# Seven block products for the second product of three feature groups, and one width for all token pairs

## The chip, the cores and the metric

The kernel runs on one core of a Trainium2 chip. The metric is the device time of one execution in microseconds; the kernel before takes 845.44 us (median of 3 runs, 845.15 to 845.78).

## What is computed

Sparse attention over 4 batches x 8 heads x 576 tokens (head size 64; half of the heads see a local window, half a strided set), then two feed-forward layers on the 2304 x 512 result, each with 2048 features, in float32:

```python
attn = np.exp(scores); attn = attn / (np.sum(attn, axis=-1, keepdims=True) + 1e-09)
x = (attn @ v), heads side by side               # 2304 x 512
h = x @ w_in;  g = h * np.clip(h + 3.0, 0.0, 6.0) / 6.0;  x = g @ w_out      # layer 1
h = x @ w_in;  g = h * np.tanh(softplus(h));              x = g @ w_out      # layer 2
```

## The kernel before, in words

Everything is held transposed: features or channels on the 128 partitions, tokens along the free dimension. `xs[0..3]` are the four 128-channel blocks of x, and later of y. A float32 operand is split into a high part (rounded to fp32r) and a low part (the rest), and each block product is a *triple* of matmuls in `mm3` (lines 985 to 987): low weights x high data, high x low, high x high.

**Order of the work.** Every instruction is first added to a `Plan` as an `Op` with its engine (or several to choose from), a cost, what it depends on, a due time and perhaps a PSUM bank. `Plan.run` then places them one by one, and the instructions are emitted in that order; each engine runs its own list in order. The constants at the top (`START`, `SOON`, `OVERLAP`, `EARLY_X`, `UNIT_Y`, `LEAD`, `BIAS`) move due times and choices in this plan.

**Stages.** Attention of 16 head pairs is mixed with the *plain steps*: the first 4 feature blocks of layer 1, by ordinary products, over all tokens in five stretches (`PLAIN`). Their y goes to DRAM (`y_kept`). From about 170 us on come 21 *units* (`build`). A unit is one of three token pairs (`TOKENS`: 2 x 288, 2 x 432 and 2 x 432 tokens) and two pairs of feature blocks (`u.fs`, two values of `fp`). Layer 1 (m = 0) has 3 groups, layer 2 (m = 1) has 4, each of 3 units.

**First product, seven products.** x as 2 x 2 blocks (two token halves, two channel halves) and w_in as 2 x 2 blocks are multiplied by Winograd's form with 7 block products instead of 8 (`PRODUCTS`: a11, a12, s2, s1, s4, s3, a22). `x_operands` makes the seven operands from `xs` in a layer's first group, splits them and keeps them in DRAM (`kept`); later groups load them (5 buffers). `decode` unpacks the packed float64 weights on VectorE (`unpack`, 512 columns at a time), makes four differences, mostly on GpSimd (line 868), and splits the pieces into `win`. A product is 2 triples (q) per fp. Partial sums stay in the bank: s2 is added onto a11's bank after a copy of it has been taken out, then s1, then s4; a22 onto s3's. So TensorE waits there for the copy or the add (lines 1179 and 1197) of the product before.

**Activation and split.** `result` (line 1108 on) applies the activation and `split` (line 763 on) makes the high part (a cast, mostly ScalarE, line 341) and the low part (a subtraction, VectorE or GpSimd, line 769) in one of 8 g tiles.

**Second product, plain.** For each token half t and each of the 4 output blocks d, one bank takes 4 triples in a row (two fp, two blocks j), then one add onto y (line 1249; line 1238 with the y kept in DRAM for layer 1's first group; a copy for layer 2's):

```python
for t in range(2):
    for d in range(KC):
        for k, (fp, j) in enumerate(chain):    # 4 triples into one bank
        ...
        o = add("dve", ..., nc.vector.tensor_tensor(y(), src(), y(), ALU.add), ...)
```

So a unit has 28 triples in the first product and 32 in the second. Banks 0 to 3 serve the first product, 4 to 7 the second (`BANKS`); in the profile and the order their names are bank_61 to 64 and bank_65 to 68. xs_75 to 78 are the four output blocks, win and wout the weights of the first and second product. Outputs of the last group go to DRAM by the SP queue as they are done.

## Time and profile before

| | us |
|---|---|
| median of 3 runs (lowest, highest) | 845.44 (845.15, 845.78) |
| the profiled execution | 847.64 |
| its span, first to last instruction | 845.9 |
| TensorE busy | 834.4 (99%) |
| VectorE busy | 588.7 (70%) |
| ScalarE busy | 421.1 (50%) |
| GpSimd busy | 225.2 (27%) |

PE is TensorE, PEld its weight loads, DVE VectorE, ACT ScalarE, POOL GpSimd, SP the queue that issues the DMAs. Matmuls are pipelined: the duration of one is longer than the distance to the next, and a full share does not say that TensorE is at its peak. A group's row ends with the time the engine stood idle just before its instructions, and whom it waited for.

### The profile page before, as it was taken

How to read it: one execution, taken by the hardware profiler on the slowest of the kernel's cores; microseconds unless marked ns; L12 is line 12 of the kernel's file. 1: busy time of each engine (PE TensorE's matmuls, PEld its weight loads, DVE VectorE, ACT ScalarE, POOL GpSimd, SP SyncE). 2: the span in 40 equal slices, each digit the busy share in tenths (PEclk: the TensorE clock that was granted, in tenths of full speed). 3: DMA queues.
4: the chain of work that ended last, by engine and by line, in shares of the span. 5: the costliest groups of instructions: out<-in, count | busy, mean ns of one | idle time of the engine just before them, and what ended most of it. 6: DMA issues, size and time to landing. Idle time of an engine off the chain costs nothing.

```text
span 845.9 us, 16976 instructions
## 1 busy us (share of the span) xinstructions
PE 834.4 (99%) x6760; PEld 774.8 (92%) x6760; DVE 588.7 (70%) x1108; ACT 421.1 (50%) x876; POOL 225.2 (27%) x237
## 2 busy tenths in 40 slices
PE   7899999999999999999999999999999999999998
PEld 4577888899999999999999999999999999999998
DVE  4688876789988868879879989766537762423423
ACT  2667766577454443544355775643353352432512
POOL 4443213424434331422304533302012300100101
PEclk8899999999999999999999999999999999999999
DMA  8866652477887876668843677757655873645731
GB/s 241 239 198 214 194 173 77 156 263 259 281 289 248 293 260 224 232 210 285 283 172 140 233 257 237 250 188 275 248 172 175 272 273 101 210 157 197 246 130 68
DMA packets 85219, 182.31 MB, mean 216 GB/s; under 512 B 6036, under 2 KB 65044, under 8 KB 85140
## 3 DMA queue, kind: packets, MB, share of 16 engines
q1 hardware_dynamic: 84480, 181.06, 63.6%
q8 instruction: 53, 0.87, 0.4%
q10 hardware_dynamic: 660, 0.16, 0.1%
q14 instruction: 26, 0.21, 0.1%
HBM read 138.74 MB, written 42.47 MB: 214 GB/s over the span
## 4 chain that ended last, share of the span: by engine, by line
PE 97%; DMA 1%; ACT 1%; issue 0%; DVE 0%; ACTq 0%; POOL 0%; SPq 0%; DVEq 0%
PE bank L985 30%; PE bank L986 30%; PE bank L987 30%; PE bank L708 2%; PE bank L1270 1%; PE bank L602 1%; PE bank L669 1%; DMA v<-in_qkv_dram 1%; DMA mk_str<-in_masks_dram 1%; PE bank L671 0%; ACT pt L341 0%; ACTq L508 0%; ACT xs L341 0%; ACT v L568 0%; POOL e L660 0%
## 5 line engine op out<-in xcount | busy, mean ns | idle before, releaser
L985 PE MATMUL bank<-x,win 128*128 128x432 f32 (+3 forms) x668 | 229.6, 344 | 0.1
L986 PE MATMUL bank<-x,win 128*128 128x432 f32 (+3 forms) x668 | 227.9, 341 | 0.0
L987 PE MATMUL bank<-x,win 128*128 128x432 f32 (+3 forms) x668 | 227.7, 341 | 0.0
L985 PE MATMUL bank<-g,wout 128*128 128x432 f32 (+3 forms) x416 | 144.2, 347 | 0.0
L987 PE MATMUL bank<-g,wout 128*128 128x432 f32 (+3 forms) x416 | 142.8, 343 | 0.0
L986 PE MATMUL bank<-g,wout 128*128 128x432 f32 (+3 forms) x416 | 142.7, 343 | 0.0
L1249 DVE TENSOR_TENSOR xs<-bank,xs 128x432 f32<-128x432 f32 (+1 forms) x120 | 66.7, 556 | 107.7 <-PE bank L987 106.8
L985 PEld LDWEIGHTS bank<-x,win 128*128 128x128 f32 x668 | 125.5, 188 | 7.0 <-POOL win L769 0.7
L986 PEld LDWEIGHTS bank<-x,win 128*128 128x128 f32 x668 | 125.8, 188 | 5.6 <-POOL x L769 0.5
L987 PEld LDWEIGHTS bank<-x,win 128*128 128x128 f32 x668 | 125.6, 188 | 5.5
L769 POOL TENSOR_TENSOR g<-t,g 128x432 fp32r<-128x432 f32 (+3 forms) x44 | 47.4, 1082 | 264.9 <-ACT g L341 165.5
L985 PE MATMUL bank<-g_late,wout 128*128 128x432 f32 (+1 forms) x336 | 113.1, 336 | 0.0
L986 PE MATMUL bank<-g_late,wout 128*128 128x432 f32 (+1 forms) x336 | 113.0, 336 | 0.0
L987 PE MATMUL bank<-g_late,wout 128*128 128x432 f32 (+1 forms) x336 | 112.9, 336 | 0.0
L987 PEld LDWEIGHTS bank<-g,wout 128*128 128x128 f32 x416 | 78.2, 188 | 4.5
L985 PEld LDWEIGHTS bank<-g,wout 128*128 128x128 f32 x416 | 78.3, 188 | 4.0
L986 PEld LDWEIGHTS bank<-g,wout 128*128 128x128 f32 x416 | 78.2, 188 | 3.5
L341 ACT COPY c<-bank 128x432 f32<-128x432 f32 (+1 forms) x42 | 20.0, 482 | 108.1 <-PE bank L987 108.1
L987 PEld LDWEIGHTS bank<-g_late,wout 128*128 128x128 f32 x336 | 63.2, 188 | 1.7
L985 PEld LDWEIGHTS bank<-g_late,wout 128*128 128x128 f32 x336 | 63.2, 188 | 1.6
L986 PEld LDWEIGHTS bank<-g_late,wout 128*128 128x128 f32 x336 | 63.2, 188 | 1.6
L769 DVE TENSOR_TENSOR g<-t,g 128x432 fp32r<-128x432 f32 (+2 forms) x60 | 39.1, 656 | 27.9 <-ACT g L341 27.5
(105 smaller groups left out, 1273.4 us busy)
## 6 DMA issues: line engine op xcount, KB each, us to landing
x<-kept SPq DMA_DIRECT2D x70, 864.0 KB, 5.0
raw<-in_wts_dram SPq DMA_DIRECT2D x64, 512.0 KB, 5.7
kept<-x SPq DMA_DIRECT2D x28, 864.0 KB, 4.7
x<-kept SPq DMA_DIRECT2D x35, 576.0 KB, 4.8
qk<-in_qkv_dram SPq DMA_DIRECT2D x14, 576.0 KB, 5.7
kept<-x SPq DMA_DIRECT2D x14, 576.0 KB, 2.8
v<-in_qkv_dram SPq DMA_DIRECT2D x14, 432.0 KB, 7.8
y<-keep SPq DMA_DIRECT2D x16, 256.0 KB, 2.1
```

The lines of the kernel that those rows point to most:

```text
L341: nc.scalar.copy(out, src)
L602: nc.tensor.matmul(banks[both[h].n][g * QN:(g + 1) * QN, slot * WK:(slot + 1) * WK], src.q[h * D:(h + 1) * D, n // 6, n % 2 * QN:(n % 2 + ...
L669: nc.tensor.transpose(banks[turned[0].n][:, j * P:(j + 1) * P], e[:, t:t + 2].rearrange("p s k -> p (s k)"), ident)
L708: nc.tensor.matmul(o[h * D:(h + 1) * D], src.v[rows, NB + others(local).index(n) if n in others(local) else i, h * D:(h + 1) * D], pt[rows ...
L769: lambda eng: engines[eng].tensor_tensor(lo(), src(), hi().bitcast(F32), ALU.subtract),
L985: nc.tensor.matmul(o, low_w, high, start=first, stop=False, skip_group_check=True)
L986: nc.tensor.matmul(o, high_w, low, start=False, stop=False, skip_group_check=True)
L987: nc.tensor.matmul(o, high_w, high, start=False, stop=last, skip_group_check=True)
L1249: "dve", dve_ns(n), lambda y=y, src=src: nc.vector.tensor_tensor(y(), src(), y(), ALU.add),
L1270: plan.filler = cleared, 3 + 4 * FILL / 2.4, lambda n: nc.tensor.matmul(banks[n][:, :FILL], zeros[:, :P], zeros, start=True, stop=True)
```

## The change

Three things change together.

1. `TOKENS` becomes 3 x (2 x 384) instead of 2 x 288, 2 x 432, 2 x 432, and `WIDE` 384; operand buffers are now without gaps. `PLAIN` becomes 512, 448, 512, 320, 512.
2. The seven products get a new order (`PRODUCTS`), and in it another use of the banks (`CHAIN`): a12 has its own bank, and a copy of it is taken first; s3 and a22 share one; a11, s2, s1 and s4 share one. The activated blocks stay in the buffers c, u, v and t instead of passing through t.
3. Groups 2 to 4 of layer 2 (`BOTH`) form the second product by seven block products too. `decode` treats their output weights like the input weights (four differences, 28 block columns). `g_operand` makes s3, s1, s2 and s4 from the activated blocks and splits seven operands per fp. Each product is then 2 triples (one per fp) for each of 2 output blocks q, in the order `SECOND`, and after each product its bank's running sum is added onto y (line 1295). A bank is used on before it is free: the next product of its chain waits for that add. Of units without it, the second token half now comes first.

The diff, cut to its core (buffers, names and the records of who uses a buffer are left out):

```diff
-TOKENS = ((0, 288), (576, 432), (1440, 432))
-WIDE = 448
-PLAIN = (512, 512, 512, 256, 512)
+TOKENS = ((0, 384), (768, 384), (1536, 384))
+WIDE = 384
+PLAIN = (512, 448, 512, 320, 512)
...
+BOTH = ((0, 0, 0), (0, 1, 1, 1))
-PRODUCTS = ("a11", "a12", "s2", "s1", "s4", "s3", "a22")
+PRODUCTS = ("a12", "a11", "s3", "s2", "a22", "s1", "s4")
+SECOND = ("a11", "s3", "s2", "a22", "s1", "a12", "s4")
+CHAIN = {"a11": "a", "s2": "a", "s1": "a", "s4": "a", "a12": "c", "s3": "b", "a22": "b"}
...
-N_OUT, N_OUT_EARLY = 4, 2
-N_X, X_FROM = 5, 3
+N_OUT, N_OUT_EARLY = 3, 2
+N_X = 5
+N_G, N_G_EARLY = 9, 6
-N_RAW, N_WA, N_T, N_F, N_S = 3, 2, 3, 2, 2
+N_RAW, N_WA, N_T, N_F = 2, 2, 3, 4
+N_S = {"c": 2, "u": 2, "v": 2}
...
-START, FIRST_PACE = 42117, 3359
+START, FIRST_PACE = 42920, 3359
-SOON = 54
+SOON = 11
-OVERLAP = 9536
-UNIT_Y, UNIT_X = -740, 15237
-LEAD = 0.6776
+OVERLAP = 14375
+UNIT_Y, UNIT_X = 6429, 15237
+LEAD = 1.0667
-BIAS = {"act": -347, "dve": 300, "pool": 0}
+BIAS = {"act": -305, "dve": 318, "pool": 0}
...
-        u.one, u.two = 7 * cost, 8 * cost
+        u.one, u.two = 7 * cost, (7 if u.both else 8) * cost
...
+        def chain_of(keys, use, before, product, evict, first_due):
...
+            banks_of = {(c, key): Bank(use) for c in "abc" for key in keys}
+            last, gone = {}, {}
+            for i, kind in enumerate(PRODUCTS if use == "h" else SECOND):
+                c = CHAIN[kind]
+                for key in keys:
+                    bank, started = banks_of[c, key], (c, key) in last
+                    deps = [*last.get((c, key), []), *gone.get((c, key), [])]
...
+                    last[c, key] = [prev]
+                    gone[c, key] = evict(i, kind, key, prev, bank, lambda bank=bank: banks[bank.n][:, :n])
...
+        def g_operand(fp, name, number):
+            if name == "s3":
+                summed(fp, "s3", "a11", "a21", ALU.subtract)
+            elif name == "s2":
+                summed(fp, "s1", "a21", "a22", ALU.add)
+                summed(fp, "s2", "s1", "a11", ALU.subtract)
+            elif name == "s4":
...
+                    lambda eng: engines[eng].tensor_tensor(x.tile(), x.tile(), y.tile(), ALU.subtract),
...
+            ops = split(n, lambda: g_tiles(slot)[0], lambda: g_tiles(slot)[1], r.tile, r.ready, old)
...
+            TO = {"a11": (0, 0), "s3": (1, 1), "s2": (1, 0), "a22": (1, 0), "s1": (1, 1), "a12": (0, 0), "s4": (0, 1)}
+            def second_evict(i, kind, q, o, bank, psum):
...
+                (t, c), ends = TO[kind], kind in ("a22", "a12", "s4")
+                return add_to_y(t, 2 * q + c, o, psum, due + UNIT_Y, bank if ends else None, kind in ("a22", "a12", "s4", "s1"))
+            before = opened["y"][-2:]
+            chain_of(range(2), "y", before, second_product, second_evict, u.at + u.one)
+            return
...
-        for t in range(2):
+        for t in (1, 0):
```

**How the order moves, TensorE.** Within the last group of layer 2, before, where the next unit's first product (x,win) stands beside a unit's second product (g_late,wout):

```order
L985 MATMUL bank_65<-g_late,wout_72 128x432
L986 MATMUL bank_65<-g_late,wout_72 128x432
L987 MATMUL bank_65<-g_late,wout_72 128x432
L985 MATMUL bank_62<-x,win_2287 128x432
L986 MATMUL bank_62<-x,win_2287 128x432
L987 MATMUL bank_62<-x,win_2287 128x432
L985 MATMUL bank_64<-x,win_69 128x432
L986 MATMUL bank_64<-x,win_69 128x432
L987 MATMUL bank_64<-x,win_69 128x432
L985 MATMUL bank_68<-g_late,wout_71 128x432
L986 MATMUL bank_68<-g_late,wout_71 128x432
L987 MATMUL bank_68<-g_late,wout_71 128x432
```

and the same place of the change:

```order
L1012 MATMUL bank_67<-g,wout_2289 128x384
L1013 MATMUL bank_67<-g,wout_2289 128x384
L1014 MATMUL bank_67<-g,wout_2289 128x384
L1012 MATMUL bank_63<-x,win_2288 128x384
L1013 MATMUL bank_63<-x,win_2288 128x384
L1014 MATMUL bank_63<-x,win_2288 128x384
L1012 MATMUL bank_67<-g,wout_71 128x384
L1013 MATMUL bank_67<-g,wout_71 128x384
L1014 MATMUL bank_67<-g,wout_71 128x384
L1012 MATMUL bank_63<-x,win_2288 128x384
L1013 MATMUL bank_63<-x,win_2288 128x384
L1014 MATMUL bank_63<-x,win_2288 128x384
```

Before, triples of the two products stand in ones and twos, with long runs of one alone elsewhere (57 matmuls of the second product, 45 of the first in a unit of this group). Now single triples of the two alternate through most of layer 2, and a bank of the second product (65, then 67) is left after two triples, one per weight buffer, for the next bank.

**How the order moves, VectorE.** The end of its list, the last unit, before (t_87 and g_late belong to the operands' split, xs_75 to 78 are the output blocks):

```order
L769 TENSOR_TENSOR g_late<-t_87,g_late 128x288
L1249 TENSOR_TENSOR xs_75<-bank_65,xs_75 128x288
L1249 TENSOR_TENSOR xs_76<-bank_68,xs_76 128x288
L1249 TENSOR_TENSOR xs_77<-bank_66,xs_77 128x288
L1249 TENSOR_TENSOR xs_78<-bank_67,xs_78 128x288
L1249 TENSOR_TENSOR xs_75<-bank_65,xs_75 128x288
L1249 TENSOR_TENSOR xs_76<-bank_68,xs_76 128x288
L1249 TENSOR_TENSOR xs_77<-bank_66,xs_77 128x288
L1249 TENSOR_TENSOR xs_78<-bank_67,xs_78 128x288
```

and of the change:

```order
L776 TENSOR_TENSOR g<-f_2293,g 128x384
L1295 TENSOR_TENSOR xs_76<-bank_68,xs_76 128x384
L1295 TENSOR_TENSOR xs_78<-bank_65,xs_78 128x384
L776 TENSOR_TENSOR g<-t,g 128x384
L1295 TENSOR_TENSOR xs_75<-bank_67,xs_75 128x384
L1295 TENSOR_TENSOR xs_77<-bank_66,xs_77 128x384
L776 TENSOR_TENSOR g<-t,g 128x384
L1295 TENSOR_TENSOR xs_75<-bank_68,xs_75 128x384
L1295 TENSOR_TENSOR xs_77<-bank_65,xs_77 128x384
L1295 TENSOR_TENSOR xs_76<-bank_67,xs_76 128x384
L1295 TENSOR_TENSOR xs_78<-bank_66,xs_78 128x384
L1295 TENSOR_TENSOR xs_75<-bank_68,xs_75 128x384
```

Before, each bank (65 to 68) is taken out once per token half, after its 4 triples, onto one output block. Now the two banks of a product are taken out after each product: 67 and 66, then 68 and 65, and so on, each onto blocks 75 and 77 or 76 and 78, with the low halves of later operands (g<-t,g) between them.

## Rows read from the trace of the kernel before

**Rows 1.** The page, parts 1 and 2: span, busy us (share) xinstructions, clock in slices.

```profile
span 845.9 us, 16976 instructions
...
PE 834.4 (99%) x6760; PEld 774.8 (92%) x6760; DVE 588.7 (70%) x1108; ACT 421.1 (50%) x876; POOL 225.2 (27%) x237
...
PEclk8899999999999999999999999999999999999999
```

**Rows 2.** Waits of TensorE, the longest two: us in total, times, longest us.

```profile
PE bank L602 <- DMA xs<-in_qkv_dram: 2.4, 2, 2.0
PE bank L708 <- issue: 2.3, 2, 1.9
```

**Rows 3.** Busy time by stretch, all engines; columns in the first row.

```profile
core 0: us, PE busy (x) PEld busy (x) DVE busy (x) ACT busy (x) POOL busy (x), PEclk, DMA share, GB/s
30.00:200.00 170.00, 167.67 (x2541) 136.85 (x2540) 135.69 (x259) 116.95 (x248) 56.22 (x51) 0.99 0.58 190
200.00:294.00 94.00, 94.00 (x547) 91.42 (x546) 83.25 (x156) 48.02 (x101) 36.84 (x35) 1.00 0.82 276
...
482.00:529.00 47.00, 47.00 (x266) 45.59 (x265) 42.57 (x77) 30.40 (x65) 13.64 (x11) 1.00 0.73 250
...
576.00:670.00 94.00, 94.00 (x541) 91.35 (x540) 57.42 (x109) 38.60 (x77) 16.66 (x19) 1.00 0.66 226
670.00:764.00 94.00, 94.00 (x503) 90.73 (x502) 39.84 (x69) 36.32 (x68) 11.47 (x11) 1.00 0.57 191
```

**Rows 4.** In order of time, TensorE, 730.2 to 768 us: first, last of 195; start, duration.

```profile
729.99 0.35 PE L985 MATMUL bank<-g,wout 128*128 128x432 f32 x1
...
767.98 0.35 PE L987 MATMUL bank<-g,wout 128*128 128x432 f32 x1
```

**Rows 5.** The same view from 830.2 us: first and last of 95 matmuls, last add.

```profile
830.03 0.29 PE L986 MATMUL bank<-g,wout 128*128 128x288 f32 x1
...
842.41 0.29 PE L987 MATMUL bank<-g_late,wout 128*128 128x288 f32 x1
...
842.74 0.46 DVE L1249 TENSOR_TENSOR xs<-bank,xs 128x288 f32<-128x288 f32 x1 [0.72 <-PE bank L987]
```

**Rows 6.** Groups by line and shape from 200 us: busy us, mean ns, idle before.

```profile
L1249 DVE TENSOR_TENSOR xs<-bank,xs 128x432 f32<-128x432 f32 x80 | 48.5, 606 | 88.6 <-PE bank L987 87.8
L868 POOL TENSOR_TENSOR w<-w 128x256 f32<-128x256 f32 x48 | 38.2, 813 | 36.2 <-DVE w L823 32.7 <-DVE wa L792 2.9
...
L341 ACT CAST g_late<-t 128x432 fp32r<-128x432 f32 x56 | 30.5, 553 | 8.7 <-DVE t L1133 7.8
...
L769 DVE TENSOR_TENSOR g_late<-t,g_late 128x432 fp32r<-128x432 f32 x43 | 26.7, 634 | 4.0 <-ACT g_late L341 3.1
...
L1249 DVE TENSOR_TENSOR xs<-bank,xs 128x288 f32<-128x288 f32 x40 | 18.2, 456 | 19.0 <-PE bank L987 19.0
...
L769 POOL TENSOR_TENSOR g_late<-t,g_late 128x432 fp32r<-128x432 f32 x13 | 16.8, 1292 | 24.4 <-ACT g_late L341 23.2 <-issue 1.2
...
L929 DVE TENSOR_TENSOR f<-f,x 128x432 f32<-128x432 f32 x5 | 2.8, 597 | 0.0
```

**Rows 7.** Output adds, low halves: ns min/median/max; then output adds alone, 576 to 670 us.

```profile
L1249 DVE TENSOR_TENSOR xs<-bank,xs x120: 445/607/610, 292.2 to 842.7; 128x432 f32<-128x432 f32 x80, 128x288 f32<-128x288 f32 x40
...
L769 DVE TENSOR_TENSOR g<-t,g x43: 445/607/1346, 210.5 to 819.5; 128x432 fp32r<-128x432 f32 x32, 128x288 fp32r<-128x288 f32 x11
...
576.00:670.00 94.00, 0.00 (x0) 0.00 (x0) 13.37 (x24) 0.00 (x0) 0.00 (x0) 1.00 0.66 226
```

**Rows 8.** DMA issues of the page, the narrow output row: KB each, median us to landing.

```profile
out_dram<-xs SPq DMA_DIRECT2D x8, 144.0 KB, 1.8
```

**Rows 9.** Busy time by stretch, instructions on a bank alone (columns without GpSimd).

```profile
200.00:294.00 94.00, 94.00 (x547) 91.42 (x546) 25.80 (x50) 11.04 (x23) 1.00 0.82 276
482.00:529.00 47.00, 47.00 (x266) 45.59 (x265) 4.64 (x8) 10.84 (x24) 1.00 0.73 250
```

**Rows 10.** Who waited for whom, from 200 us: us in total, times, longest.

```profile
DVE xs L1249 <- PE bank L987: 106.8, 81, 4.1
```

More of the change, by code (lines that the diff above doesn't have):

```diff
@@ L849, in decode_plain, with plain_out @@
         in_use[0, fp] = [[]] * len(W_PIECES)
-        out_use[0, fp] = []
+        out_use[0, fp] = [[]] * len(W_PIECES)
+    both = {}
+    for u in units:
+        both.update({(u.m, fp): u.both for fp in u.fs})
+    def plain_out(slot):
+        return wout_t[slot][:, :4 * DM].rearrange("p (f h c) -> p f h c", f=2, h=2)
     def decode(m, fp):
@@ new lines, in activated @@
+                if not psum:
+                    by.use.append(o)
+            else:
+                old = at.old if psum else []
+                o = add("act", act_ns(n, psum), lambda: nc.scalar.activation(at.tile(), src(), AF.Mish), [*deps, *old], frees=frees)
+            r.ready = [o]
+            blocks[fp, to] = r
+        def chain_of(keys, use, before, product, evict, first_due):
+            nonlocal due
+            due = first_due
+            banks_of = {(c, key): Bank(use) for c in "abc" for key in keys}
[5 more added lines that the diff above has]
+                    deps = [*last.get((c, key), []), *gone.get((c, key), [])]
+                    if i == 0:
+                        deps.extend(before)
+                    prev = None
+                    parts = product(i, kind, key)
+                    for x, (more, emit) in enumerate(parts):
+                        due += cost
+                        prev = add(
+                            "pe", cost, lambda emit=emit, bank=bank, first=not started and x == 0, last=x == len(parts) - 1: emit(banks[bank.n][:, :n], first, last),
+                            [prev, *deps, *more], due=due, bank=None if started or x else bank,
+                        )
+                        if not started and x == 0:
+                            opened[use].append(prev)
+                    last[c, key] = [prev]
+                    gone[c, key] = evict(i, kind, key, prev, bank, lambda bank=bank: banks[bank.n][:, :n])
@@ new lines, in build, with first_product, emit @@
+        x_now, snaps = {}, {}
+        def first_product(i, kind, fp):
+            if kind not in x_now:
+                x_now[kind] = x_operands(u, kind, due - EARLY_X)
+            x_slot, x_parts, x_use = x_now[kind]
+            piece, block = W_OF[kind]
+            step = 1 if piece else 2
+            w_slot, w_ready = in_ready[m, fp]
+            parts = []
+            for q in range(2):
+                def emit(o, first, last, q=q, k=block + q * step):
+                    w = win_t[w_slot].rearrange("p (h b c) -> p h b c", h=2, c=P)
+                    x = x_view(x_slot)
+                    mm3(o, w[:, 0, k], w[:, 1, k], x[:, 0, q], x[:, 1, q], first, last)
+                parts.append(([*w_ready[piece], *x_parts[q]], emit))
+            return parts
@@ new lines, in first_evict @@
+        def first_evict(i, kind, fp, o, bank, psum):
+            x_now[kind][2].append(o)
+            if u.closes:
+                in_use[m, fp][W_OF[kind][0]].append(o)
+            if kind in ("a12", "s3", "s2"):
+                at = snaps[kind, fp] = take({"a12": "c", "s3": "v", "s2": "u"}[kind])
+                o = add(None, copy_ns(n, True), lambda eng: copy(eng, at.tile(), psum()), [o, *at.old], frees=bank if kind == "a12" else None)
+                at.ready = [o]
+                return [o]
+            if kind == "s4":
+                activated(fp, "a12", psum, [o], take("t"), bank)
+                return []
+            of, to = {"a11": ("a12", "a11"), "a22": ("s2", "a21"), "s1": ("s3", "a22")}[kind]
+            at = snaps[of, fp]
+            o = add(
+                "dve", dve_ns(n), lambda: nc.vector.tensor_tensor(at.tile(), psum(), at.tile(), ALU.add),
+                [o, *at.ready], frees=bank if kind == "a22" else None,
+            )
+            activated(fp, to, at.tile, [o], at)
+            return [o]
@@ new lines, in build, with summed @@
+        before = opened["h"][-len(u.fs):]
+        chain_of(u.fs, "h", before, first_product, first_evict, due)
+        sums = {}
+        def summed(fp, name, x, y, op):
+            x, y = blocks[fp, x], blocks[fp, y]
+            r = take("f")
+            o = add(
+                None, plain_ns(n), lambda eng: engines[eng].tensor_tensor(r.tile(), x.tile(), y.tile(), op), [*x.ready, *y.ready, *r.old],
+                lock=("dve", "pool"),
+            )
+            r.ready = [o]
+            x.use.append(o)
+            y.use.append(o)
+            blocks[fp, name] = r
```

432 lines of the change are left out of this document (207 added, 225 removed).

## The prediction

> **What bounds the kernel now.** I read the page's busy shares and slices first. TensorE is busy 834.4 of 845.9 us, and its granted clock is at the upper level (2.4 GHz, shown as 9s) in all but the first two slices [rows 1]. A busy TensorE can still be a waiting one, so the second view is the list of its waits: seven short entries, led by 2.4 us on a line of the attention, and none on the block products' lines (985 to 987) [rows 2]. The third view, busy time by stretch, says where: 2.3 us of idle TensorE between 30 and 200 us, and 0.00 in the stretches after that, also where VectorE is busy 83.25 of 94 us or 42.57 of 47 [rows 3]. So from 200 us to the last unit's end the time is the number of matmuls times the spacing of their starts; a change is worth what it does to these two numbers, as long as no other engine becomes later than TensorE.
>
> The spacing is not the duration in the rows (matmuls are pipelined), so I take it from start times. For 432 columns 195 matmuls lie between 729.99 and 767.98 us: 37.99 / 194 = 195.8 ns [rows 4]. For 288 columns the last 95 start from 830.03 to 842.41 us: 12.38 / 94 = 131.7 ns [rows 5].
>
> **The change, part by part.**
>
> *Fewer matmuls.* In a unit (one token pair, two pairs of feature blocks) the first product is 28 triples of matmuls before and after. The second was 2 token halves x 4 output blocks x 4 = 32 triples; in groups 2 to 4 of layer 2 it becomes 7 block products x 2 x 2 = 28. That is 4 triples, 12 matmuls, less in each of 9 units: 108. The instruction order shows it: 5560 TensorE instructions become 5451, the odd one being a filler.
>
> *Width.* All units now have 384 columns. No row shows a 384-wide matmul. Between the two measured widths a straight line gives 131.7 + 96 x (195.8 - 131.7) / 144 = 174.4 ns. Bounds: the 288 row plus 96 columns at the clock's 2.4 GHz is 171.7; the 432 row less 48 such columns is 175.8. I take the line, since 384 lies between the rows. A group of three units was 180 x 131.7 + 360 x 195.8 = 94.2 us; as 540 x 174.4 it is 94.2 again. So the widths by themselves give nothing in the four groups that keep 32 triples (the opening stage's widths, 512 + 448 + 320 for 512 + 512 + 256, add to the same columns, also nothing). The three others take 504 x 174.4 = 87.9, 6.3 us less each: **18.9 us**. Over all 3672 such matmuls the bounds shift this by -9.9 to +5.1 us.
>
> The Trainium skill, "TensorE: Matmul & The Clock Gate", section "Back-to-back issue gap", gives an isolated spacing of the columns over 2.4 GHz plus 2.5 ns, so 182.5 ns at 432 and 122.5 at 288. This trace does not agree: 195.8 and 131.7. By the page the sum would be an estimated -17.5 us instead of -18.9.
>
> *VectorE.* What the saved matmuls cost elsewhere: a unit of those nine evicts 14 sums of PSUM onto the output instead of 8, adds or subtracts 8 times in SBUF, and splits 14 operands instead of 8 into high and low. By row: an add out of PSUM takes 606 ns at 432 columns and 456 at 288, so 556 at 384; an SBUF sum 597 and a low half 634 at 432, less the same 50 at 384: 547 and 584 [rows 6]. Of the 72 sums the new order puts 42 on VectorE and 30 on GpSimd, of the low halves about six in ten. For a group (three units) that decodes the next one's weights, the nearest stretch is 576 to 670 us with 57.42 us of VectorE [rows 3]: of its output adds, 13.37 us [rows 7], 42 x 0.556 = 23.4 are to come, +10.0; sums 14 x 0.547 = +7.7; low halves 11 x 0.584 = +6.4. Sum 81.5 of 87.9 us, 93%. The fullest stretch of before is 42.57 of 47, 91%, without one idle TensorE [rows 3]. I cost it at **nothing**: hidden under TensorE, but with 2 points less air than any row shows.
>
> *ScalarE and GpSimd.* Six more casts a unit at under 0.55 us [rows 6] bring ScalarE from 38.60 in 94 us to some 50 of 88, the wider output weights' casts among it: nothing. GpSimd had 16.66 in that stretch; 10 sums and 7 low halves at 1.15 (1292 ns at 432, by columns), 8 more differences of the output weights at 0.81 [rows 6] and two low halves of that same width make about 44 of 88: nothing, by itself.
>
> *The returns to a bank.* A block product adds onto a bank whose partial sum VectorE has just to take out, so TensorE waits for that add. In the second product (a11, s3, s2, a22, s1, a12, s4 on two banks each) a bank is used again after three other products of 6 matmuls: 18 x 0.174 = 3.1 us when nothing else runs, twice that where the first product of the next unit alternates with it by triples, as the order has it nearly everywhere in layer 2. The add needs 0.56 us. The first product of before has the same kind of return with one product between (s3, then a22, after an add into v), 6 x 0.196 = 1.2 us, 42 times, and no wait on lines 985 to 987 shows. Its new order moves s3 and a22 apart; s1 to s4 remain one product apart, now with an add in place of a copy. Cost: **nothing**, unless VectorE is over 2.5 us late.
>
> *The end.* The last unit has nothing beside it: 96 matmuls of 288 before, 84 of 384 after; both are in the sum. After the last matmul (842.41 + 0.29) come one add and the output's transfer, to 845.9 [rows 1, 5]. The add grows by 0.10 us; the transfer goes from 144 KB, landing in 1.8 us [rows 8], to 192 KB, so by 0 to 0.6 us; I take 0.1: **+0.2 us**.
>
> *The opening.* Attention and the plain steps keep their work; the order moves some triples. What can be lost or won there is what was idle between 30 and 200 us, 2.3 us [rows 3]: nothing, +-2.3. Operands kept in DRAM move the same bytes, now in one run per partition; no wait on them showed on TensorE.
>
> **Sum:** -18.9 + 0.2 = -18.7. The profiled execution took 847.64 us (span 845.9 and 1.7 around it), 2.2 above the median of 845.44. So 847.6 becomes 828.9 and the median **826.7 us**.
>
> **Rivals.**
>
> *A, the port.* VectorE instructions with two SBUF inputs and GpSimd get in each other's way: low halves of g on VectorE have a minimum of 445, a median of 607 and a maximum of 1346 ns, while output adds, which read PSUM, never pass 610 [rows 7]. Work of the first kind plus GpSimd is (83.25 - 25.80) + 36.84 = 94.3 of 94 us from 200 to 294 us [rows 3, 9]. In a decoding group after the change it is 81.5 - 60 x 0.556 + 44 = 92.1 of 87.9. If the two could not overlap at all, 4.2 us a group would be lost, in the two groups that decode: 8.4 us, 835. Against it: from 482 to 529 us the same sum is 42.57 - 4.64 + 13.64 = 51.6 of 47 [rows 3, 9] and TensorE still never waited, so the spans overlap or hold waiting. The Trainium skill, "SBUF — State Buffer", section "Who interferes with whom", calls this an exclusive lock, held for a whole instruction, between GpSimd and a VectorE instruction with two SBUF inputs. That is rival A; the spread of g's rows agrees with it. Chance 0.13.
>
> *B, slower.* VectorE falls so far behind that the returns to a bank wait: 5 dependent products x 2 banks x 9 units = 90 returns. The saving is gone when they wait 0.21 us on average (18.7 / 90); with a wait of one add each, 0.56, the kernel takes 845.4 - 18.7 + 50 = 877. For it: 93% on VectorE, and an instruction of 1.35 us can stand in front of an add. Against: 81 of the 120 output adds found VectorE idle, waiting for TensorE for 106.8 us [rows 10], and the slack is 3.1 us or more. Chance 0.06.
>
> *C, the price.* The change does drop 108 matmuls, the order shows it; but 384 columns may cost the upper bound (+5.1) and the opening may slip (+2.3): 834. Nothing in the rows points there, except that the spacing had to be interpolated. Chance 0.07.
>
> **How the numbers follow.** Forecast 0.74, with a range of its own from 822 (half of the lower bound on spacing) to 831 (most of the upper, or waits of a few us). With C it reaches 834 (0.81 in all); A's 835 and B are left out. About 0.2% (1.7 us) is what a measurement of this kernel can tell from no change. Faster: forecast, A and C, 0.94; slower is B but for its threshold, 0.05; same, B near its threshold, 0.01.
>
> **What would show it.** Spacing of 384-wide matmuls at 174 ns, so 94 us for a group of 32 triples and 88 for one of 28; TensorE without waits after 200 us; VectorE above 90% in the second and third groups of layer 2, its output adds still mostly waiting for TensorE. Wrong, if TensorE waits appear on VectorE's xs adds (B) or at splits of g (A), or if the spacing is over 176 ns (C).

## The result, and the profile after

| | kernel before | changed kernel |
|---|---|---|
| median of the runs | 845.3 us (845.15 to 845.78) | 822.9 us (822.62 to 824.57) |
| profiled run: span | 845.9 us | 821.1 us |
| TensorE, instructions | 6760 | 6650 |
| VectorE, busy share | 70% | 82% |

The ratio is 0.9738 (95% interval 0.9721 to 0.9755): 2.6% faster, 22.4 us by the medians. The forecast was 18.7 us and 826.7; the range of 822 to 834 holds the result. The direction and the main term came as forecast. How well the sum's other terms did is another matter, and most of what follows.

The page of the changed kernel, parts 1 and 2, answers to [rows 1]:

```profile
span 821.1 us, 17043 instructions
...
PE 808.3 (98%) x6650; PEld 771.0 (94%) x6650; DVE 676.0 (82%) x1238; ACT 447.2 (54%) x941; POOL 325.9 (40%) x324
...
PEclk9999999999999999999999999999999999999999
```

All three other engines have more to do and TensorE less. It is still the bound, as the view of its waits says (us in total, times, longest; beside these rows stand only those of the attention and of the fillers, which are matmuls of zeros that the plan puts where TensorE would stand idle in the first 60 us):

```profile
PE bank L1013 <- DVE g L776: 1.1, 2, 0.8
...
PE bank L1012 <- POOL win L776: 0.2, 1, 0.2
PE bank L1012 <- ACT c L348: 0.2, 1, 0.2
```

Line numbers have moved: 1012 to 1014 are the block products' lines (985 to 987 before), 1295 the output add, 776 the low half of a split, 348 the cast, 1237 and 1255 the sums of the second product's operands. There are waits on those lines now, where [rows 2] had none, but they are small, and they are on the splits of g, not on the output adds. The same stretches as in [rows 3], for the changed kernel:

```profile
core 0: us, PE busy (x) PEld busy (x) DVE busy (x) ACT busy (x) POOL busy (x), PEclk, DMA share, GB/s
30.00:200.00 170.00, 168.59 (x2542) 142.95 (x2542) 143.65 (x264) 119.28 (x246) 54.82 (x47) 1.00 0.60 197
200.00:294.00 94.00, 93.80 (x539) 92.98 (x538) 85.52 (x157) 47.27 (x100) 31.76 (x29) 1.00 0.81 287
...
576.00:670.00 94.00, 94.00 (x544) 94.00 (x543) 85.45 (x141) 50.23 (x107) 61.31 (x57) 1.00 0.68 233
670.00:764.00 94.00, 93.49 (x538) 92.80 (x537) 85.74 (x152) 48.99 (x103) 53.85 (x52) 1.00 0.65 223
```

From 576 to 670 us VectorE went from 57.42 to 85.45 us and GpSimd from 16.66 to 61.31, and TensorE was idle for none of the 94. Who waited for whom, to be held against [rows 10]:

```profile
DVE xs L1295 <- PE bank L1014: 48.3, 67, 3.0
```

67 of 174 output adds still waited for TensorE, against 81 of 120 before. So the sign "output adds still mostly waiting for TensorE" did not come: VectorE was behind it more often than not, but nearly always in time.

The spacing of 384-wide matmuls is read as in [rows 4], from a stretch in time order, first and last of 1553 without a wait between them:

```profile
449.21 0.34 PE L1014 MATMUL bank<-g,wout 128*128 128x384 f32 x1
...
718.22 0.36 PE L1012 MATMUL bank<-x,win 128*128 128x384 f32 x1
```

269.01 us / 1552 = 173.3 ns. I had taken 174.4.

**Where the 24.8 us between the two spans lie.** 108 matmuls fewer at 173.4: -18.7 (the rows are 110 fewer: two are fillers). The remaining 3672 in the changed kernel cost 173.4 ns each instead of the old mix (132.3 ns for 288 and 195.6 for 432, means after 200 us; weighted 1 to 2 that is 174.5): 1.1 x 3672 = -4.0. Late starts after 200 us, each counted by how much more than 173 ns it came behind the start before: about +2.9. Behind the last matmul: +0.2. What is left, some -5, lies before 200 us. These five terms are what the experiments took apart.

### The profile page after: what moved, and what is told of

The parts are those of the page before. It is cut to its first block, busy times and chain, and to the rows that moved or that the text cites. A ratio compares the mean times of both kernels' runs of the same rounds, so it can differ in the third digit from the quotient of the medians.

```text
span 821.1 us, 17043 instructions
## 1 busy us (share of the span) xinstructions
PE 808.3 (98%) x6650; PEld 771.0 (94%) x6650; DVE 676.0 (82%) x1238; ACT 447.2 (54%) x941; POOL 325.9 (40%) x324
## 4 chain that ended last, share of the span: by engine, by line
PE 89%; DVE 4%; DMA 3%; ACT 1%; POOL 1%; issue 1%; ACTq 0%; SPq 0%; DVEq 0%
PE bank L1012 29%; PE bank L1013 28%; PE bank L1014 28%; PE bank L715 2%; DMA raw<-in_wts_dram 1%; PE bank L609 1%; DMA v<-in_qkv_dram 1%; PE bank L676 1%; DMA mk_str<-in_masks_dram 1%; POOL w L898 1%; PE bank L1382 0%; DMA qk<-in_qkv_dram 0%; DVE wa L816 0%; DVE xs L1295 0%; DVE wa L811 0%
## 5 line engine op out<-in xcount | busy, mean ns | idle before, releaser
L1012 PE MATMUL bank<-x,win 128*128 128x384 f32 (+3 forms) x668 | 227.8, 341 | 0.4 <-POOL win L776 0.2
L1013 PE MATMUL bank<-x,win 128*128 128x384 f32 (+3 forms) x668 | 226.2, 339 | 0.1
L1014 PE MATMUL bank<-x,win 128*128 128x384 f32 (+3 forms) x668 | 226.1, 338 | 0.0
L1012 PE MATMUL bank<-g,wout 128*128 128x384 f32 (+3 forms) x512 | 175.7, 343 | 0.0
L1013 PE MATMUL bank<-g,wout 128*128 128x384 f32 (+3 forms) x512 | 174.2, 340 | 1.1 <-DVE g L776 1.1
L1014 PE MATMUL bank<-g,wout 128*128 128x384 f32 (+3 forms) x512 | 174.0, 340 | 0.0
L1295 DVE TENSOR_TENSOR xs<-bank,xs 128x384 f32<-128x384 f32 x174 | 95.2, 552 | 49.5 <-PE bank L1014 48.3
L1013 PEld LDWEIGHTS bank<-g,wout 128*128 128x128 f32 x512 | 96.1, 188 | 3.0 <-DVE g L776 1.1
L1014 PEld LDWEIGHTS bank<-g,wout 128*128 128x128 f32 x512 | 96.1, 188 | 2.3
L1012 PEld LDWEIGHTS bank<-g,wout 128*128 128x128 f32 x512 | 96.1, 188 | 2.0
L898 POOL TENSOR_TENSOR w<-w 128x256 f32<-128x256 f32 x80 | 68.2, 871 | 70.1 <-DVE w L830 69.0
L1013 PE MATMUL bank<-g_late,wout 128*128 128x384 f32 x204 | 68.1, 334 | 0.0
L1012 PE MATMUL bank<-g_late,wout 128*128 128x384 f32 x204 | 68.1, 334 | 0.0
L1014 PE MATMUL bank<-g_late,wout 128*128 128x384 f32 x204 | 68.1, 334 | 0.0
L776 POOL TENSOR_TENSOR x<-xs,x 128x512 fp32r<-128x512 f32 (+3 forms) x17 | 21.1, 1244 | 63.7 <-ACT x L348 52.9
L816 DVE SCALAR_TENSOR_TENSOR wa<-raw,wa 128x512 uint32<-128x512 uint32 x64 | 45.8, 723 | 0.3
L776 POOL TENSOR_TENSOR win<-w,win 128x256 fp32r<-128x256 f32 (+1 forms) x25 | 29.1, 1170 | 40.6 <-ACT win L348 34.9
L348 ACT CAST win<-w 128x512 fp32r<-128x512 f32 (+1 forms) x56 | 31.6, 567 | 22.8 <-DVE w L830 14.6
```

The lines of the kernel that those rows point to most:

```text
L348: nc.scalar.copy(out, src)
L776: lambda eng: engines[eng].tensor_tensor(lo(), src(), hi().bitcast(F32), ALU.subtract),
L816: lambda: nc.vector.scalar_tensor_tensor(ai, high, 0xC0000000, ai, ALU.bitwise_and, ALU.bitwise_or),
L898: lambda eng: engines[eng].tensor_tensor(of[out], of[x], of[y], ALU.subtract), [*on[x], *on[y]], lock=("dve", "pool"),
L1012: nc.tensor.matmul(o, low_w, high, start=first, stop=False, skip_group_check=True)
L1013: nc.tensor.matmul(o, high_w, low, start=False, stop=False, skip_group_check=True)
```

## The experiments

All ratios are to the kernel before, on the same chip; it took medians of 846.2 to 847.2 us on the chips below, so ratios are the fairer comparison. "Columns by 200 us" adds up the widths of all block-product matmuls that start before 200 us; 1,000 columns are 0.45 us.

### The products by themselves

**No group by seven** (`e1_no_seven`): the changed kernel with the old second product everywhere, all else new.

```diff
-BOTH = ((0, 0, 0), (0, 1, 1, 1))
+BOTH = ((0, 0, 0), (0, 0, 0, 0))
```

> The change without its seven-product second product: all groups keep 32 triples, the widths, the product order and the constants stay new. Theory (time = matmuls x spacing, the rest hidden): 108 matmuls of 173.4 ns come back, 18.7 us, less the 0.5 to 2 us of waits that VectorE's new work made: 839.5 to 841.5 us. Rival (a good part of the 22 us came from elsewhere: order, widths, opening): under 836 us.

Measured: 841.1 us, ratio 0.9923 (0.9898 to 0.9948), span 839.4. This is what its theory expected. So the seven products of three groups are worth 0.0185 of 847, 15.7 us, with 2.6 us of uncertainty from the two intervals; the two spans differ by 18.3. 108 x 173.4 ns less 1.3 us of added waits is 17.4. The same run shows that 6.5 us come from the rest of the change.

**Two groups by seven** (`e3_two_groups`): only the last two.

```diff
+BOTH = ((0, 0, 0), (0, 0, 1, 1))
```

> The change with seven products in the second product of the last two groups only. Theory: 36 matmuls come back, +6.2 us, less up to 1 us of waits: 828 to 829.5 us. Rival (VectorE or the shared port gives part of the saving back in the stretch that decodes weights): the group costs as much as it gives, under 826 us.

Measured: 829.3 us, ratio 0.9789 (0.9768 to 0.9810), span 826.5: between the two as expected. By the spans, 839.4, 826.5 and 821.1: two groups give 12.9 us and the third 5.4. At 36 matmuls each it would be 12.5 and 6.2.

**All four groups of layer 2 by seven** (`e4_all_l2`): one group more than the change.

```diff
+BOTH = ((0, 0, 0), (1, 1, 1, 1))
```

> Seven products in the second product of all four groups of layer 2. Theory: 36 matmuls less, -6.2 us, as long as VectorE has air in the first group, where it also makes the operands of x: 817 to 818 us. Rival (VectorE was at 43 of 47 us in that stretch before, so the new work has no room): TensorE waits on output adds or splits, 821 us or slower.

Measured: 837.7 us, ratio 0.9891 (0.9871 to 0.9910), some 13 us slower than the changed kernel by the ratios, although it has 36 matmuls less. This is where the cover of VectorE ends. Its longest waits, then the stretches of the added group:

```profile
PE bank L1013 <- DVE g L776: 7.0, 4, 3.2
PE bank L1012 <- DVE win L776: 4.6, 3, 2.6
...
PE bank L1013 <- DVE g_late L776: 1.3, 2, 1.0
PE bank L1012 <- POOL win L776: 1.1, 2, 0.6
```

```profile
482.00:529.00 47.00, 45.97 (x265) 45.65 (x264) 44.42 (x87) 33.61 (x77) 16.58 (x14) 1.00 0.50 202
529.00:576.00 47.00, 40.68 (x216) 39.13 (x214) 42.30 (x74) 26.70 (x57) 23.27 (x26) 0.89 0.73 252
```

VectorE is busy 44.42 and 42.30 of 47 us (in the changed kernel 39.61 and 32.24). Adding the 24.1 us that the prediction priced for a group to that kernel's 71.85 gives an estimated 96 us of work for the 88 us that such a group would then last, 8 us too much, and TensorE waits for splits of g and win. Waits of 3 us then cost more than themselves: the granted clock of the second stretch is 0.89, because TensorE ran at 1.2 GHz for 10 us, from the end of one such wait at 546.5 us over a second that ended at 551.3; and once more for 3.4 us behind a wait that ended at 644.4.

### The widths

**Only the widths** (`e2_width`): the kernel before with all token pairs 384 + 384.

```diff
-TOKENS = ((0, 288), (576, 432), (1440, 432))
+TOKENS = ((0, 384), (768, 384), (1536, 384))
-    spare = [x[:, 2 * TOKENS[0][1]:] for x in xs]
+    spare = [x[:, S:] for x in xs]
```

> The kernel before with token pairs of 2 x 384 and nothing else (the attention's spare buffers begin at token 576). Theory (384 columns are cheaper per column than 288 and 432 mixed: 173.4 against 174.4 ns by the line, over 3780 matmuls): 841 to 842 us, spacing 173 to 174 ns. Rival 1 (the straight line of the prediction): 845 us, spacing 174.4. Rival 2 (the tight spacing comes from operand buffers without gaps, which this kernel does not have: pitch 448 for 384): spacing of 174.5 or more, 845 us or slower.

Measured: 843.6 us, ratio 0.9964 (0.9946 to 0.9981): 3.0 us for the widths alone, by the spans 4.8. The absolute time is above the expected one as the kernel before is on this chip (847.2). The spacing (first and last of 3677 starts) is 637.18 / 3676 = 173.3 ns:

```profile
200.06 0.33 PE L985 MATMUL bank<-x,win 128*128 128x384 f32 x1
...
837.24 0.33 PE L986 MATMUL bank<-g_late,wout 128*128 128x384 f32 x1
```

Here the operands' slots keep their old pitch of 448 elements, so it isn't the closer packing of the changed kernel's buffers that makes 173.3.

**Three widths in one run** (`e7_widths`): the kernel before with pairs of 352, 384 and 416.

```diff
-TOKENS = ((0, 288), (576, 432), (1440, 432))
+TOKENS = ((0, 352), (704, 384), (1472, 416))
```

(The line of `spare` is as in `e2_width`.)

> The kernel before with token pairs of 352, 384 and 416 columns a half, all else as before. It gives the spacing of starts at three widths in one execution. Theory (what a matmul takes over its columns at 2.4 GHz grows with the width: 11.7 ns at 288, 13.4 at 384, 15.8 at 432): 159.5 at 352, 173.4 at 384, 188.3 at 416, so 521 ns for the three. Rival (the straight line from 288 to 432 holds but for 384): 160.2, 173.4 and 188.7 ns. Third (over 384 columns something else begins, as the spread at 432 suggests): 352 and 384 tight within 2 ns, 416 spread over 5 ns or more. Time by any of them: 842 to 846 us, against 845 to 847 for the kernel before.

Measured: 847.6 us, ratio 1.0007 (0.9996 to 1.0018): above the 842 to 846 expected. First and last of 128 (at 352), 90 and 96 matmuls in stretches of one width:

```profile
821.21 0.32 PE L985 MATMUL bank<-x,win 128*128 128x352 f32 x1
...
841.50 0.32 PE L986 MATMUL bank<-g_late,wout 128*128 128x352 f32 x1
...
407.76 0.34 PE L985 MATMUL bank<-x,win 128*128 128x384 f32 x1
...
423.21 0.33 PE L987 MATMUL bank<-g,wout 128*128 128x384 f32 x1
...
721.75 0.35 PE L985 MATMUL bank<-x,win 128*128 128x416 f32 x1
...
739.65 0.35 PE L987 MATMUL bank<-g_late,wout 128*128 128x416 f32 x1
```

159.8, 173.6 and 188.4 ns in these stretches (161.0 in other long ones at 352); 160.6, 174.5 and 188.2 as the mean over everything after 200 us, with the changes between widths. The means add to 523.3 ns, against 520.1 for three times 384: x 1260 matmuls of each width, 4.0 us, as much as the widths gave in the change; by the ratios this run is 3.6 us behind `e2_width`. At 352 and 416 the straight line from 288 to 432 (160.2, 188.7) is met within a nanosecond, so neither the curve of the first theory nor a change of behaviour above 384 is shown; only 384 lies below the line, by 0.8 to 1.1 ns. It is also the only one whose starts are even: with 384 throughout, nine in ten lie between 172 or 173 and 174 ns, and so they do here in the stretch above (171 to 179 with the changes between widths); 352 has 156 to 165 and 416 183 to 191 in this run, 432 had 189 to 203 and 288 126 to 136 before. Why 384 is even isn't settled.

### The opening

**Once more** (`e6_after`): the changed kernel itself.

> The changed kernel itself once more, beside the other runs of this group, as their base and as a test of what in its profile comes again. Theory (the waits and the lead at 200 us belong to the order of the work): 822 to 825 us, the 1.1 us wait near 449 us on a split of g on VectorE again, the 384-wide spacing 173 to 174 ns, and 269,000 to 271,000 columns of block products started by 200 us. Rival (they belong to that one execution): waits at other places, and a lead at 200 us that differs by more than 2,000 columns (about 1 us).

Measured: 824.0 us (822.09 to 825.14), ratio 0.9734 (0.9716 to 0.9752), 270,336 columns by 200 us (269,952 in the first profile), the wait near 448 us again at 1.1 us, the one near 751 again at 0.6. These belong to the order of the work.

**The opening's widths** (`e8_plain`): `e2_width` with the new widths of the plain steps.

```diff
-PLAIN = (512, 512, 512, 256, 512)
+PLAIN = (512, 448, 512, 320, 512)
```

> The kernel before with all token pairs 384 + 384 wide and the opening's widths of the changed kernel (512, 448, 512, 320, 512). With pairs of 384 alone it stood 3.0 us below the kernel before on the same chip (0.9964), with the changed kernel's order and buffers too, but no second product by seven, 6.5 us below (0.9923). Theory (the opening's widths carry the rest): 0.992 to 0.994, with 267,000 or more columns started by 200 us. Rival (the new order of the products and the kept operands carry it): 0.996 to 0.997, with 263,000 or fewer.

Measured: 852.0 us, ratio 1.0072 (1.0055 to 1.0089). Both theories missed: these widths cost 9 us, by the ratios, against `e2_width`. 248,064 columns by 200 us against its 260,352 are 5.5 us, and a wait of 1.7 us on VectorE stands just behind 200 us. From 80 to 120 us TensorE was busy for only 35.69 of 40 us, and its granted clock fell to 1.2 GHz twice, for 3.4 us each (88.4 to 91.8 and 112.3 to 115.7), each time behind idle time (1.3 us until 86.75, 2.5 until 111.3). With the constants of before, the opening's widths are a loss.

**The planner's old constants** (`e5_old_consts`): the changed kernel with six of them put back.

```diff
-START, FIRST_PACE = 42920, 3359
+START, FIRST_PACE = 42117, 3359
-SOON = 11
+SOON = 54
-OVERLAP = 14375
-UNIT_Y, UNIT_X = 6429, 15237
-LEAD = 1.0667
+OVERLAP = 9536
+UNIT_Y, UNIT_X = -740, 15237
+LEAD = 0.6776
-BIAS = {"act": -305, "dve": 318, "pool": 0}
+BIAS = {"act": -347, "dve": 300, "pool": 0}
```

> The changed kernel with six of the planner's constants (START, SOON, OVERLAP, UNIT_Y, LEAD, BIAS) as before the change; products, widths and buffers stay. Theory (TensorE's matmuls set the time, and the constants only keep the small waits small): the same 6450 or so matmuls at 173.4 ns, and waits on splits of g or on win that add 2 to 10 us: 825 to 833 us. Rival (VectorE has room enough for any order that keeps dependences): within 1.5 us of the changed kernel.

Measured: 836.4 us, ratio 0.9882 (0.9867 to 0.9897): 12.4 us slower than the changed kernel beside it, 3 more than the upper end of the expectation. 260,352 columns by 200 us instead of 270,336: 4.5 us. The rest is in waits: late starts after 200 us add up to 11.4 us, against 2.3 in the changed kernel beside it, spread over many releasers:

```profile
PE bank L1012 <- ACT c L348: 3.0, 3, 1.4
PE bank L1013 <- DVE g L776: 2.2, 2, 1.2
PE bank L1012 <- DVE win L776: 1.6, 1, 1.6
...
PE bank L1012 <- POOL win L776: 0.5, 1, 0.5
```

**Half of them** (`e9_start`: START, SOON, OVERLAP and LEAD old; `e10_rank`: UNIT_Y and BIAS old; the lines as above).

> The changed kernel with START, SOON, OVERLAP and LEAD as before the change; UNIT_Y and BIAS stay new. All six old gave 836.4 us, 12.4 above the changed kernel: about 4.4 us of that by 200 us (260,352 columns started there, against 270,336), 8 in waits after it. Theory (LEAD and OVERLAP place the first steps' work, so these four carry the opening): at most 264,000 columns by 200 us, few waits behind: 827 to 831 us. Rival (UNIT_Y and BIAS, which choose among what is ready, carry both): within 2 us of the changed kernel.

> The other half: the changed kernel with UNIT_Y and BIAS as before the change; START, SOON, OVERLAP and LEAD stay new. Theory (UNIT_Y ranks an add onto the output against the splits of the next operands, so the old value brings the waits after 200 us): 269,000 or more columns by 200 us, and 5 to 9 us of waits after: 828 to 833 us. Rival (they were harmless with the other four new): within 2 us of the changed kernel.

Measured: 830.9 us (0.9805, 0.9783 to 0.9827) and 837.6 us (0.9891, 0.9864 to 0.9917). The first came in time and columns as its theory had it, but not with "few waits behind": late starts after 200 us add up to 8.2 us. The second did not: it lost the opening as well (263,424 columns, where 269,000 were expected), its late starts add up to 13.3 us, and alone it is no better than all six together. So there is no opening half and no later half: the constants act as one set, and either half of the old set undoes the lead. Over all runs:

| by 200 us | fillers | columns |
|---|---|---|
| kernel before | 36 | 258,912 |
| `e2_width`, `e7_widths` | 36 | 260,352, 260,928 |
| `e8_plain` | 36 | 248,064 |
| `e5_old_consts`, `e9_start`, `e10_rank` | 36 | 260,352, 262,272, 263,424 |
| changed kernel, again | 34 | 269,952, 270,336 |
| `e1_no_seven`, `e3_two_groups`, `e4_all_l2` | 34 | 268,032, 270,336, 267,264 |
| `e11_sums_pool`, `e12_sums_dve` (below) | 34 | 267,264, 272,640 |

Every kernel with the whole new set is 3,800 columns or more ahead of every other. (The new set in the kernel before was not run: what is shown is that the lead goes when half of the set or all of it is taken back.) How can that be, with 2.3 us of idle TensorE between 30 and 200 us in [rows 3] and 1.4 in the changed kernel? Most of the lead is there at 80 us: 51,072 columns against 43,520, with about as many of the attention's 2,464 matmuls started (1,484 and 1,460). The row of 30 to 80 us, and the fillers from 30 to 200 us, kernel before:

```profile
30.00:80.00 50.00, 47.67 (x1023) 34.59 (x1022) 40.41 (x81) 32.23 (x64) 19.78 (x16) 0.97 0.67 206
```

```profile
L1270 PE MATMUL bank<-xs 128*128 128x512 f32 x16 | 8.5, 657 | 0.0
```

and the changed kernel:

```profile
30.00:80.00 50.00, 48.59 (x1057) 36.92 (x1058) 43.95 (x81) 35.36 (x71) 20.13 (x17) 1.00 0.75 228
```

```profile
L1382 PE MATMUL bank<-xs 128*128 128x512 f32 x13 | 6.3, 600 | 0.0
```

All of TensorE's idle time between 30 and 200 us lies in this row: 2.33 and 1.41 us. But its busy time is not all work. The fillers that start after 30 us (16 before, 12 in the changed kernel, where the row's 13th began earlier) take 8.2 and 6.0 us, each counted to the next start; over all runs, 12 to 14 with the whole new set and 15 or 16 without it. And the granted clock is 0.97 on average before, because it was at 1.2 GHz from 36.7 to 40.1 us; in the changed kernel it was at 2.4 GHz in all of that time. Idle time and fillers make 3.1 of the 5 us; the lower clock makes at most an estimated 1.7 (half of 3.4). The rest isn't placed.

In the pair that differs by the constants alone, `e5_old_consts` and the changed kernel beside it, TensorE was idle for 3.77 and 1.29 us between 30 and 200 us, and the fillers took 7.9 and 5.8. Together that is 4.6 us, where the columns say 4.5. The fall of the clock isn't needed there, and it comes and goes between runs: `e1_no_seven` has one at 54.4 us and is at 268,032 columns all the same.

### The sums between the products

**All on GpSimd** (`e11_sums_pool`), **all on VectorE** (`e12_sums_dve`): in the changed kernel the plan has 42 of 72 on VectorE. The edit, for lines 1237 and 1255 both (`"dve"` and `dve_ns` in the other):

```diff
-                None, plain_ns(n), lambda eng: engines[eng].tensor_tensor(r.tile(), x.tile(), y.tile(), op), [*x.ready, *y.ready, *r.old],
+                "pool", pool_ns(n), lambda eng="pool": engines[eng].tensor_tensor(r.tile(), x.tile(), y.tile(), op), [*x.ready, *y.ready, *r.old],
```

> The changed kernel with all 72 sums and differences of the second product's operands on GpSimd (the plan had 42 of them on VectorE). That takes some 42 x 0.55 = 23 us off VectorE and adds some 42 x 1.15 = 48 to GpSimd over the nine units. In the changed kernel VectorE's instructions with two SBUF inputs took 51.5 us more after 200 us than if each had its shape's shortest time (28.4 in the kernel before), and the wait near 751 us follows two of them of 1.4 us. Theory (what TensorE still waits for is such a stretched instruction beside GpSimd): the stretch grows though VectorE has fewer instructions, waits on splits of g grow: 824 to 832 us. Rival (VectorE is simply full, and any work off it helps): stretch and waits shrink, 820 to 823 us.

> The other end: all 72 sums and differences of the second product's operands on VectorE. It takes 30 x 1.1 = 33 us off GpSimd and adds 30 x 0.55 = 16.5 to VectorE, so 5.5 a group: 91 of 94 us in the two groups that decode (85.5 now). With all of them on GpSimd the time was 829.0 (ratio 0.9786, changed kernel 0.9734), by waits on splits of g whose sums had come late, while the stretch of VectorE's instructions stayed at 51.1 us. Theory (a sum of 0.55 us in place of 1.1 shortens the chain to the next g, and VectorE still has 3 us of air a group): 821 to 824 us, ratio 0.970 to 0.974, stretch below 51 us. Rival (at 91 of 94 us VectorE is too full, as in the run with layer 2's first group by seven too): waits on splits of g and win of 3 us or more, 826 to 834 us, ratio above 0.976.

Measured: 829.0 us (0.9786, 0.9768 to 0.9804) and 828.8 us (0.9800, 0.9773 to 0.9827): both slower than the changed kernel, by some 5 us. The plan answered each edit by moving low halves the other way: with all sums on GpSimd VectorE has 35 instructions less than in the changed kernel, not 42 (six more low halves, and one more besides); with all sums on VectorE it has 15 more, not 30 (15 fewer low halves), as the page of that run counts:

```profile
PE 811.2 (98%) x6650; PEld 773.0 (94%) x6650; DVE 680.3 (82%) x1253; ACT 448.1 (54%) x941; POOL 307.0 (37%) x309
```

With all on GpSimd the time falls into its theory's range, but not for its reason: the stretch (what VectorE's instructions with two SBUF inputs took over their shape's shortest) stayed at 51.1 us. In order of time, TensorE waited 1.8 us until 725.04 for the split at 724.44; VectorE, then GpSimd:

```profile
722.90 0.42 DVE L811 TENSOR_SCALAR wa<-wa 128x512 uint32<-128x512 uint32 x1
723.23 0.68 DVE L830 SCALAR_TENSOR_TENSOR w<-raw,wa 128x512 uint32<-128x512 uint32 x1
723.83 0.68 DVE L816 SCALAR_TENSOR_TENSOR wa<-raw,wa 128x512 uint32<-128x512 uint32 x1
724.44 0.55 DVE L776 TENSOR_TENSOR g_late<-f,g_late 128x384 fp32r<-128x384 f32 x1
```

```profile
718.35 2.44 POOL L1237 TENSOR_TENSOR f<-f,c 128x384 f32<-128x384 f32 x2
```

The sums were done at 720.8. VectorE then worked through eight steps of decoding, with no idle time, before it came to the split. After 1.4 us of work at 2.4 GHz TensorE's clock then fell, too; starts stood 320 ns apart for 3.4 us, which cost some 1.6 us more:

```profile
726.50:729.90 3.40, 3.40 (x13) 0.50 0.80 249
```

In the other run it is the same place in the program: TensorE waits for the low half of win at 723.71, whose weights VectorE had decoded only by 722.7, in a queue of nine such steps and two sums without idle time; VectorE, then TensorE:

```profile
722.64 0.68 DVE L816 SCALAR_TENSOR_TENSOR wa<-raw,wa 128x512 uint32<-128x512 uint32 x1
723.24 0.55 DVE L1237 TENSOR_TENSOR f<-u,v 128x384 f32<-128x384 f32 x1
723.71 0.68 DVE L776 TENSOR_TENSOR win<-w,win 128x512 fp32r<-128x512 f32 x1
```

```profile
724.45 0.65 PE L1012 MATMUL bank<-x,win 128*128 128x384 f32 x1 [3.31 <-DVE win L776]
724.90 0.52 PE L1013 MATMUL bank<-x,win 128*128 128x384 f32 x1
725.22 0.52 PE L1014 MATMUL bank<-x,win 128*128 128x384 f32 x1
725.54 0.52 PE L1012 MATMUL bank<-x,win 128*128 128x384 f32 x1
```

After the wait of 3.3 us starts are 320 ns apart: 1.2 GHz, for 3.4 us. In the same run VectorE's busy time from 576 to 670 us was 84.37 us, not the 91 expected: 12 more sums lie in that stretch, but six other instructions fewer, four of them low halves, and with GpSimd at 45.66 instead of 61.31 us the stretch of VectorE's instructions fell by some 4 us there (from 51.5 to 47.6 over all after 200 us). So the rival's sign (a wait of over 3 us, 828.8) came without its reason: VectorE wasn't fuller. The plan, made anew for each edit, had come out in another order, and that lost 5 us; so neither run tells what a sum on one engine or the other is worth by itself.

## Why the prediction was right, and where not

- *Fewer matmuls*, -18.9 of the forecast's 18.7: **right**. 108 at 173.4 ns are 18.7 (the trace has two fillers fewer besides, where the prediction counted one); with and without the seven products the measured difference is 15.7 (by ratios, 2.6 either way) to 18.3 us (by spans).
- *Width*, "the widths by themselves give nothing": **mis-sized**. The line gave 174.4 ns and 384 takes 173.4, inside the bounds of 171.7 to 175.8. 1.1 ns less times 3672 is 4.0 us of gain; the widths alone measured 3.0 (`e2_width`). By the isolated spacing in the Trainium skill, "TensorE: Matmul & The Clock Gate", section "Back-to-back issue gap", 384 columns would take an estimated 162.5 ns; the trace does not agree, 173.3.
- *VectorE*, "nothing: hidden under TensorE, with 2 points less air than any row shows": the price was right (93% forecast; 85.45 and 85.74 of 94 us, 91%), and that it was nearly nothing too: late starts after 200 us sum to 2.9 us, 1.5 of them at two splits of g. What failed is the view behind it, that a share of busy time tells how much air there is. `e4_all_l2` lost 13 us with VectorE busy for 86.7 of 94 us in the added group, and `e11_sums_pool`, `e12_sums_dve` and `e5_old_consts` show 4 us and more lost at a share in these two stretches that is no higher.
- *ScalarE and GpSimd*: 50.23 us against "some 50", right. GpSimd took 61.31 and 53.85 of 94 us, more than 44 of 88. The plan gave it more (57 and 52 instructions, where the working has some 46), and they were longer (differences 871 ns on average, 813 in [rows 6]). It cost nothing by itself, as said.
- *The returns to a bank*, "nothing": **right**; no wait of TensorE on an output add appears in the changed kernel.
- *The opening*, "nothing, +-2.3": **wrong**, and the step that failed is its bound: what was idle between 30 and 200 us. TensorE's busy time also held fillers, 8.2 us of them after 30 us, and, in the profiled execution, 3.4 us at 1.2 GHz. Some 5 us were won (4.5 by `e5_old_consts`): 0.9 of idle time, 2.2 of fillers and the rest not placed. They were won only with the whole new set of constants. The diff showed these constants and I gave them no price.
- *The end*, +0.2: right, 3.16 us from the last matmul's end to the span's before, 3.38 after.
- *The profiled run*, 2.2 us above the median before: the changed kernel's stands at its median (822.89 and 822.92), so the spans moved by 24.8 us and the medians by 22.4. Part of the 5 us of the opening, then, may belong to that one execution of before.

By the spans the sum was 6.1 us short (-4.0 and about -5 missed on one side, +2.9 on the other); the 2.2 us taken off for the profiled run made up for some of it, and the number came out 3.8 us too high.

**Rival A** (the port) lost as a price and was seen as a mechanism. Its sum for 576 to 670 us is now (85.45 - 33.05 on a bank) + 61.31 = 113.7 of 94 us with no idle TensorE, so adding the two engines' rows says nothing: rows hold waiting. But VectorE's stretch after 200 us rose from 28.4 to 51.5 us, and one of the two waits stands right behind two stretched instructions. Around it, VectorE, GpSimd and TensorE in the changed kernel:

```profile
748.82 1.41 DVE L1237 TENSOR_TENSOR f<-u,v 128x384 f32<-128x384 f32 x1
750.16 1.37 DVE L776 TENSOR_TENSOR g<-f,g 128x384 fp32r<-128x384 f32 x1
751.45 0.55 DVE L1237 TENSOR_TENSOR f<-f,c 128x384 f32<-128x384 f32 x1
```

```profile
747.37 2.44 POOL L776 TENSOR_TENSOR wout<-w,wout 128x256 fp32r<-128x256 f32 x2
749.78 1.33 POOL L776 TENSOR_TENSOR g_late<-v,g_late 128x384 fp32r<-128x384 f32 x1
```

```profile
751.67 0.41 PE L1013 MATMUL bank<-g,wout 128*128 128x384 f32 x1 [0.32 <-DVE g L776]
```

Two instructions of a 0.55 us shape take 1.4 us each while GpSimd works on SBUF, the next, behind GpSimd's last, takes 0.55 again, and TensorE starts 0.49 us late. The Trainium skill, "SBUF — State Buffer", section "Who interferes with whom", has this as an exclusive lock; the rows agree in kind. **Rival B** (late output adds) did not occur in the change, nor in `e4_all_l2`: there the splits are late, not the adds. Of all the runs only `e9_start` has a wait on an output add, of 0.2 us. **Rival C** fell: the spacing was lower, not higher.

None of the kernels tried beats the changed one. What was not tried is another set of the planner's constants fitted to a different share of sums, or to layer 2's first group by seven; nor the new constants, or the new order of the products, in the kernel before.

## What to carry to other kernels

A count of instructions times their spacing, on the engine that is never idle, forecast the main term (18.9 us, where 15.7 to 18.3 were measured); get that spacing at the very width that will run, since one nanosecond in 173 was worth 3.7 us here. Don't take an engine's idle time as the bound of what can be won there. Its rows overlap (after 200 us the changed kernel's late starts add up to 2.9 us, its idle time to 1.5), and busy time can hold fillers or a lower clock: count the work that has started by a given moment (51,072 against 43,520 columns at 80 us). And when a change comes with new constants of a scheduler, price them as a part of their own: here taking them back cost 12.4 of the 22.8 us by the medians, so the same products under the old set gained less than half.

## What the runs showed of the hardware

- Starts of 384-wide matmuls in a stream of that width are even, nine in ten within 2 ns; those of 288, 352, 416 and 432 spread over 8 to 14 ns. A run with three widths costs some 4 us more than one with 384 throughout, at the same number of columns (3.6 by the ratios, 4.0 by the spacings).
- TensorE's clock fell to 1.2 GHz for 3.4 us after a wait of 3.3 us (`e12_sums_dve`), and for 10 us around two of 3 us (`e4_all_l2`). At that level a 384-wide start takes 320 ns instead of 173, so a wait of 3.3 us cost about 1.6 us more. It fell for 3.4 us after shorter waits as well: one of 1.8 us (`e11_sums_pool`), and one of 1.6 us with one of 1.0 us 2.6 us after it (`e10_rank`). Single waits of 1.9 us (`e9_start`) and 1.6 us (`e5_old_consts`) and the 1.1 us gap of the changed kernel had no such effect, so the length of a wait alone does not tell.
- VectorE instructions with two SBUF inputs stretch beside GpSimd's work on SBUF: from 0.55 to 1.4 us each at 749 to 751 us. Over all after 200 us their stretch was 28.4 us with GpSimd busy for 27% of the kernel before, and 51.5 with 40% in the changed one. GpSimd's differences took 871 ns on average, 813 before; what made them longer was not taken apart.
